# Routing the last tokens of a fused attention, dense and expert kernel in halves, one turned by TensorE

## The chip, the cores and the metric

The kernel runs on 1 core of one Trainium2 chip. The metric is the device time of one execution in microseconds; the number given is the median of several runs. A span is the time from the first to the last instruction of the profiled execution.

## What is computed

Three layers in a row. Attention over 2 batches x 8 heads x 768 tokens of 64, masked to keys in the query's hash bucket; then a dense layer `g = h * sigmoid(1.702 h)`, `g @ w_out` on 1536 tokens of 512 (hidden 2048); then a layer of 8 experts, two for each token:

```python
logits = x @ w_gate
noise_scale = np.log1p(np.exp(x @ w_noise))
noisy_logits = logits + noise_scale * noise
top2 = np.argpartition(-noisy_logits, 2, axis=1)[:, :2]
...
        h = np.maximum(x[mask] @ w1[e], 0.0)
        out[mask] += top2_w[mask, k, None] * (h @ w2[e])
```

The second and third layer's matmuls are done as three f16 products each (high and low parts).

## The kernel before

**Chunks and steps.** The 1536 tokens form 6 chunks of 256 (`B * NCH`, 3 a batch), each two tiles of 128 (`CT`). The program is one long list of steps. In the first part a step g does one attention tile (g under `NU` = 96) and, for a finished chunk, one of 16 pieces of the dense layer: 8 pieces h (24 matmuls of 256 columns) and 8 pieces px (12 matmuls of 512), 4 for each tile. Chunk 4 is in step 85 + i, chunk 5 in step 99 + i. A table by step (`at`, `start`, `soon`, with offsets from PARAM) says which side work is emitted in which step: loads, weight splits, routing. In a step, `start` work comes first, then the eviction of the last piece (th on ACT and DVE), the matmuls of this piece (`moe_pe`), the split of gt, and last the `at` work, whose generators are run in turns, one instruction each. Every engine runs its own instructions in exactly the order in which they are emitted; nothing overtakes.

**Routing.** When px of a tile is done, ACT and DVE write it as high and low parts to `xr` (L485, L494). `r_t` (L567) turns a tile by a DMA transpose on SP's queue into `xrt`. `route` (L572) is a generator: 16 small matmuls pz, a copy zc on ACT, some 35 DVE operations on tiles of 128 x 16 or less with four exponentials on ACT between them, the choice of two experts (top, ix), the one-hot mk, two matmuls pp that count the tokens ahead of each in its expert (cum carries the sum over chunks), and slot numbers si. It ends with four indirect DMAs on POOL's queue (L685), a tile and choice each, that scatter the rows of `xr` with their metadata into `slots` in DRAM. It yields between instructions, and `yield 1` where the result goes to another engine. `next` or `piece` takes it to the next `yield 1`: before, one or two a step. `reserve` (L693) sees to it that the first 256 slots of expert 0 hold only tokens of chunks 0 to 4, so that they can be loaded before chunk 5 is routed.

**Experts.** In the second part a step x is one item of a list: "1" a group of 12 matmuls into ph (`l1`, L790; the first weights times a block of hidden units), with its eviction to ht by ACT and DVE one step later, or "2" a tile of 24 matmuls into py (`l2`, L813). Expert 0 (`EA` = 1) has two parts: slots 0 to 255, then 256 to 399. `e_load` (L749) loads a part's tokens by a transposing DMA from `slots` into xg, on SP's queue, and the metadata mt; `e_meta` (L769) turns mt into weights and row numbers by six or more small DVE operations. `w12_load` and `w12_split` (L724, L735) load an expert's weights in 512 KB blocks and split them on ACT and DVE. The order on PE is: 8 groups ph and 2 tiles py of expert 0's first part, 8 groups ph of its second part, the first group ph of expert 1, then py and ph in turns to the end.

**Chunk 5 before.** Its routing is not in the table: from x = 2 on, up to 8 instructions of its generator are emitted ahead of each expert step (`QX` = 8, `QS` = 2), and it has to be done at x = 7 (`QE`), where expert 0's second part is loaded:

```python
    for x in range(-4, len(seq) + 2):
        for _ in range(PARAM["QX"]):
            if x >= PARAM["QS"]:
                next(gen, None)
```

Names of tiles in the rows are those of the program; L numbers are lines of the kernel before.

Of the kernel before, what the change touches and what calls it, by code (L numbers as in the profile page):

```python
# [7 lines left out]
F32 = mybir.dt.float32  # L8
# [10 lines left out]
DM = H * D  # L19
# [37 lines left out]
PARAM.update(KA={(0, 0, 0): -15, (0, 0, 1): -6, (0, 1, 0): -5, (0, 1, 1): -4, (0, 2, 0): -1, (0, 2, 1): 1, (0, 3, 0): 4, (0, 3, 1): 5, (1, 0, 0): 37, (1, 0, 1): 39, (1, 1, 0): 44, (1, 1, 1): 46, (1, 2, 0): 42, (1, 2, 1): 51, (1, 3, 0): 47, (1, 3, 1): 51}, QA={(0, 0, 0): -15, (0, 0, 1): -3, (0, 0, 2): 1, (0, 0, 3): 3, (0, 1, 0): 8, (0, 1, 1): 9, (0, 1, 2): 17, (0, 1, 3): 21, (0, 2, 0): 24, (0, 2, 1): 28, (0, 2, 2): 30, (0, 2, 3): 33, (1, 0, 0): 37, (1, 0, 1): 41, (1, 0, 2): 47, (1, 0, 3): 52, (1, 1, 0): 57, (1, 1, 1): 56, (1, 1, 2): 60, (1, 1, 3): 69, (1, 2, 0): 72, (1, 2, 1): 69, (1, 2, 2): 80, (1, 2, 3): 84}, VA={(0, 0, 0): -1, (0, 0, 1): -3, (0, 1, 0): -1, (0, 1, 1): -1, (0, 2, 0): 0, (0, 2, 1): 0, (0, 3, 0): -1, (0, 3, 1): -2, (1, 0, 0): -1, (1, 0, 1): -1, (1, 1, 0): 2, (1, 1, 1): -4, (1, 2, 0): -3, (1, 2, 1): -3, (1, 3, 0): 2, (1, 3, 1): -2}, PV={(0, 0, 0): 4, (0, 0, 1): 5, (0, 0, 2): 6, (0, 0, 3): 5, (0, 1, 0): 6, (0, 1, 1): 4, (0, 1, 2): 4, (0, 1, 3): 5, (0, 2, 0): 5, (0, 2, 1): 5, (0, 2, 2): 5, (0, 2, 3): 6, (1, 0, 0): 4, (1, 0, 1): 5, (1, 0, 2): 4, (1, 0, 3): 5, (1, 1, 0): 5, (1, 1, 1): 5, (1, 1, 2): 5, (1, 1, 3): 6, (1, 2, 0): 6, (1, 2, 1): 4, (1, 2, 2): 4, (1, 2, 3): 4}, RA={0: 18, 1: 18, 2: 19, 3: 24, 4: 18}, W=[(g,1) for g in [-6, -4, -3, -1, 0, 0, 1, 1, 2, 4, 4, 7, 8, 8, 9, 10, 11, 12, 13, 14, 15, 16, 16, 17, 18, 20, 20, 22, 22, 23, 23, 24]], EC=lambda g:'AA', LE=lambda nc:nc.sync, HI=lambda g:'AAAA'[g%4], LO=lambda g:[0, 0, 0, 1, 0, 0, 0, 1][g%8]==1, S1=[8, 8, 8, 8, 8, 11, 13, 22], ST={0: 4, 1: 4, 2: 5, 3: 4, 4: 5, 5: 3}, NG=28, WS=lambda i:'PAAA'[i%4], HE=lambda nm,b:'DPDD'[2*(nm=='k')+b], OE=lambda nm,b:'DTDD'[2*(nm=='k')+b], SC=lambda nm,b:'DADD'[2*(nm=='k')+b], R1=2, I0=26, IS=1, O0=56, OS=1, GM=100, BK=3, OH=3, QX=8, QS=2, QE=7, VF=0, T0=12, T1=17, EL=10, WX=5, WL=2, PC=2, GW=2, E0=8, WB=2)  # L57
# [3 lines left out]
def fused(ctx: ExitStack, tc: tile.TileContext, q, k, v, proj, w_in, w_out, w_gate, w_noise, noise,  # L61
# [505 lines left out]
    def r_t(ci, t):  # L567
        xrt = rt.tile([128, 2 * HP, 128], U16, name="xrt")
        rst[ci, "xt", t] = xrt.bitcast(F16)
        nc.sync.dma_start_transpose(xrt, mst[ci, "xr"][:, t, :2 * DM])  # L570

    def route(ci):  # L572
        b, cc = divmod(ci, NCH)
        pz = psr.tile([128, CT, 4 * E], F32, name="pz", tag="pb", bufs=1)
        for t in range(CT):
            xrt = rst.pop((ci, "xt", t))
# [13 lines left out]
        w = rt.tile([128, 6, CT, E], F32, name="rw", bufs=1)  # L590
# [22 lines left out]
        nc.vector.tensor_tensor(y, y, noi[:, b, cc * CT:(cc + 1) * CT, :], op=OP.mult)  # L613
# [547 lines left out]
```

## Time and profile before

| | |
|---|---|
| three runs | 814.7, 815.28, 812.03 us; median 814.7 |
| the profiled execution | 813.59 us, span 811.9 us |
| busy, share of the span | PE 705.7 us (87%), DVE 536.6 (66%), ACT 446.0 (55%), POOL 270.3 (33%) |
| mean granted TensorE clock | 0.956 of full speed |
| costliest group | L460, PE, h: 1152 matmuls, 142.5 us |

The profile is of one execution. Each row of its timeline gives start, duration, engine, line, operation, output and inputs, and in brackets how long the engine had been idle and on what it waited. The chain of waits follows the work that ended last backwards, at each step to what released it. PEclk is the clock granted to TensorE as a share of 2.4 GHz; 0.50 is its other level, 1.2 GHz.

### The profile page before, as it was taken

The numbers are of one execution on the slowest core, as the hardware profiler recorded it, in microseconds if no ns is written. First come the engines' busy times: TensorE is split into PE (matmuls) and PEld (weight loads), VectorE is DVE, ScalarE is ACT, GpSimd is POOL, SyncE is SP. The second block draws the span as 40 slices with busy tenths as digits, with TensorE's granted clock in tenths as the row PEclk, the third lists the DMA queues.
The fourth block names the chain that finished last, engine by engine and source line by source line (L and its number), as shares of the span: only waits on it lengthen the run. The fifth ranks groups of instructions, "written<-read, shape, count | busy, mean of one in ns | idle before, by whom it ended". The sixth has DMA issues, their size and how long they took to land.

```text
span 811.9 us, 14841 instructions
## 1 busy us (share of the span) xinstructions
PE 705.7 (87%) x5398; PEld 436.7 (54%) x5399; DVE 536.6 (66%) x1338; ACT 446.0 (55%) x859; POOL 270.3 (33%) x305
## 2 busy tenths in 40 slices
PE   1576578988988888889899999897999999999995
PEld 1353346645754565468468667365545545555452
DVE  8999789996896789569778724563635436354320
ACT  3678767766876686467567615342534435344220
POOL 6444646561444054304212223231130211302113
PEclk9979679899999999999999999998999999999998
DMA  8999679999999999996796650858768768587313
GB/s 220 216 250 236 177 173 188 253 265 237 179 163 205 166 189 194 210 171 105 119 182 119 111 182 12 208 197 210 169 173 216 161 181 206 128 203 156 79 17 45
DMA packets 267998, 139.46 MB, mean 172 GB/s; under 512 B 225232, under 2 KB 243728, under 8 KB 267920
## 3 DMA queue, kind: packets, MB, share of 16 engines
q1 hardware_dynamic: 261904, 125.31, 69.5%
q0 software_dynamic: 6016, 13.16, 9.0%
q8 instruction: 43, 0.70, 0.4%
q14 instruction: 35, 0.29, 0.1%
HBM read 61.48 MB, written 23.20 MB: 104 GB/s over the span
## 4 chain that ended last, share of the span: by engine, by line
PE 45%; DVE 23%; DMA 15%; issue 7%; ACT 6%; POOL 3%; SPq 1%; POOLq 0%; ACTq 0%; DVEq 0%
PE ph L799 16%; PE py L830 14%; PE h L460 5%; PE px L471 5%; DMA et<-er 5%; DVE er L323 4%; DVE e L266 3%; DMA qt<-qsb 3%; ACT er L314 2%; DMA q<-in_q_dram 2%; DMA qt<-qsa 2%; DVE wf L431 2%; DVE wraw L434 2%; ACT e L275 2%; PE s L254 2%
## 5 line engine op out<-in xcount | busy, mean ns | idle before, releaser
L460 PE MATMUL h<-xt,wi 128*128 128x256 f16 x1152 | 142.5, 279 | 6.9 <-DVE th L490 3.0
L799 PE MATMUL ph<-xg,ew 128*128 128x400 f16 (+2 forms) x864 | 136.4, 322 | 8.8 <-DMA xg<-slots 8.7
L743 DVE SCALAR_TENSOR_TENSOR ew<-w,ew 128x1024 f16<-128x1024 f32 x64 | 77.9, 1225 | 82.2 <-ACT ew L742 82.1
L471 PE MATMUL px<-wo,gt 128*128 128x512 f16 x576 | 131.0, 379 | 0.5 <-DVE th L490 0.5
L460 PEld LDWEIGHTS <-wi 128*128 128x128 f16 x1152 | 113.7, 100 | 29.8 <-issue 9.8
L830 PE MATMUL py<-ew,ht 128*128 128x512 f16 x576 | 125.8, 379 | 0.0
L847 POOL DMA_INDIRECT out_dram<-yo,ti x32 | 54.0, 1687 | 204.8 <-ACT yo L840 197.9
L254 PE MATMUL s<-kt,qt 128*128 128x512 f16 (+1 forms) x384 | 86.9, 348 | 35.0 <-DVE mx L266 28.0
L799 PEld LDWEIGHTS <-ew 128*128 128x128 f16 x864 | 83.7, 102 | 59.9 <-issue 6.8
L275 ACT ACTIVATE e<-e,mx 128x768 f32<-128x768 f32 x96 | 89.4, 931 | 28.7 <-DVE mx L266 22.0
L505 POOL TENSOR_TENSOR gt<-th,gt 128x512 f16<-128x512 f32 x48 | 59.3, 1236 | 123.5 <-ACT gt L504 123.0
L266 DVE CUSTOM_DVE_ANT_0 e<-s,zero 128x768 f32<-128x768 f32 x96 | 90.6, 948 | 6.5 <-PE pt L293 2.6
L323 DVE SCALAR_TENSOR_TENSOR er<-e,mx,er 128x768 f16<-128x768 f32 x68 | 73.5, 1083 | 28.9 <-ACT er L314 28.3
L830 PEld LDWEIGHTS <-ht 128*128 128x128 f16 x576 | 56.3, 98 | 67.0
L471 PEld LDWEIGHTS <-gt 128*128 128x128 f16 x576 | 54.9, 98 | 62.6 <-issue 0.8
L314 ACT ACTIVATE er<-e,mx 128x768 f16<-128x768 f32 x68 | 63.1, 930 | 40.7 <-DMA et<-er 26.7
L809 ACT ACTIVATE ht<-ph 128x400 f16<-128x400 f32 (+2 forms) x72 | 33.5, 466 | 72.8 <-PE ph L799 72.7
L254 PEld LDWEIGHTS <-qt 128*128 128x128 f16 x384 | 36.9, 102 | 64.0 <-issue 37.4
L742 ACT ACTIVATE ew<-w 128x1024 f16<-128x1024 f32 x64 | 66.4, 1048 | 3.7 <-DMA w<-in_moe_w_dram 3.4
L840 ACT ACTIVATE yo<-py,wv 128x512 f32<-128x512 f32 x24 | 16.5, 686 | 90.2 <-PE py L830 57.3
L810 DVE SCALAR_TENSOR_TENSOR ht<-ph,ht 128x400 f16<-128x400 f32 (+2 forms) x72 | 37.6, 523 | 36.7 <-ACT ht L809 36.7
L368 PE MATMUL pv<-et,vt 128*64 128x256 f16 x720 | 50.3, 281 | 5.4 <-DMA et<-er 5.4
(197 smaller groups left out, 932.3 us busy)
## 6 DMA issues: line engine op xcount, KB each, us to landing
w<-in_moe_w_dram SPq DMA_DIRECT2D x64, 512.0 KB, 4.7
wraw<-in_moe_w_in_dram SPq DMA_DIRECT2D x16, 512.0 KB, 4.5
wraw<-in_moe_w_out_dram SPq DMA_DIRECT2D x16, 512.0 KB, 4.2
slots<-blank SPq DMA_DIRECT2D x6, 1032.0 KB, 6.8
v<-in_v_dram SPq DMA_DIRECT2D x24, 192.0 KB, 4.1
out_dram<-zeros SPq DMA_DIRECT2D x13, 256.0 KB, 3.3
k<-in_k_dram SPq DMA_DIRECT2D x16, 192.0 KB, 3.8
q<-in_q_dram SPq DMA_DIRECT2D x24, 128.0 KB, 3.1
```

What stands on the lines that cost most here:

```text
L254: nc.tensor.matmul(ps[:, n0 * 128:n1 * 128], qt[:, s, h, t, :], kt[:, s, h, n0:n1, :].rearrange("p c t -> p (c t)"), start=(s == 0), stop= ...
L266: nc.vector.tensor_tensor_reduce(e32, st[g]["ps"][:, :S], zero.to_broadcast([128, S]), -0.125, TOP, op0=OP.add, op1=OP.min, accum_out=mx[: ...
L275: nc.scalar.activation(e32, e32, AF.Exp, scale=-1.0, bias=st[g]["mx"][:, 1:2], accum_out=sms[b, cc, hp][:, 2 * h + t:2 * h + t + 1] if g < ...
L314: nc.scalar.activation(er[:, 0], st[g]["e"], AF.Copy, scale=r)
L323: nc.vector.scalar_tensor_tensor(er[:, 1], d["e"], d["mx"][:, 3:4], er[:, 0], op0=OP.mult, op1=OP.subtract)
L460: nc.tensor.matmul(ph[:, a, :], wi[ws][:, d, f0:f0 + 128], xt[:, d, xs, :], start=(d == 0 and ws == 0 and xs == 0), stop=(d == HP - 1 and ...
L471: nc.tensor.matmul(px, gts[ci, f // 2][:, gs, f % 2, t * 128:t * 128 + 128], wo[ws][:, f, :], start=(f == 0 and gs == 0 and ws == 0), stop ...
L505: nc.gpsimd.tensor_tensor(gt[:, 1], th, gt[:, 0], op=OP.subtract)
L742: nc.scalar.activation(hi, x, AF.Copy, scale=SW1 if j == 0 else SW2)
L743: nc.vector.scalar_tensor_tensor(lo, x, SW1 if j == 0 else SW2, hi, op0=OP.mult, op1=OP.subtract)
L799: nc.tensor.matmul(ph[:, :c1 - c0], w[:, ws, d * FE + f * 128:d * FE + f * 128 + 128], xg[e, p][:, xs * HP + d, :], start=(d == 0 and ws = ...
L830: nc.tensor.matmul(py, ht[:, f, hs, t * 128:t * 128 + 128], w[:, ws, f * DM:(f + 1) * DM], start=(i == 0), stop=(i == n - 1))
```

## The change

Four things are changed.

1. **Chunk 4's routing takes more hops a step.** With r0 = 103 it was taken one hop a step from step 103 to 107, its last part (from the exponential d on) in step 110, `reserve` in 111. Now `hops` takes three in step 103, four in 104, one in 105; the last part with the scatters comes in step 107, `reserve` in 108. `e_load` of expert 0 is called one step earlier (112), and `e_meta` later (x = 4, not step 115).
2. **Chunk 5 is routed in two halves** of one tile each, two generators `gen0` and `gen`, each with its own matmuls, about as many DVE and ACT operations as a whole chunk, and two scatters. `gen0` starts in step 114; its small tiles are cut out of one tile zt. `gen` is emitted from x = 3, in turns with the rest of `gen0`.
3. **The second half's rows are turned by TensorE**: 8 transposes (128x128, f16) into a PSUM tile xp, emitted at x = 1 behind the second ph group, and two copies of 128x512, one on ACT, one on DVE. The DMA transpose of that tile is gone from SP's queue.
4. In PARAM, `QX` goes from 8 to 10 and `QS` from 2 to 3 (a line that is not shown).

The core of the diff; in `route` all other lines change only in that `CT` becomes `T`, `rt.tile` becomes `small`, and a slice is cut to the half:

```diff
-        nc.sync.dma_start_transpose(xrt, mst[ci, "xr"][:, t, :2 * DM])
-
-    def route(ci):
+        xr = mst[ci, "xr"][:, t, :2 * DM]
+        if (ci, t) != LAST:
+            nc.sync.dma_start_transpose(xrt, xr)
+            return
+        xp = psum2.tile([128, 2 * HP, 128], F16, name="xp", bufs=1)
+        for i in range(2):
+            for d in range(i * HP, i * HP + HP):
+                nc.tensor.transpose(xp[:, d], xr[:, d * 128:d * 128 + 128].bitcast(F16), ident)
+            o = xrt[:, i * HP:i * HP + HP].bitcast(F16)
+            if i == 0:
+                nc.scalar.activation(o, xp[:, :HP], AF.Copy)
+            else:
+                nc.vector.tensor_copy(o, xp[:, HP:])
+
+    LAST = B * NCH - 1, CT - 1
+
+    def route(ci, ta=0, tb=CT):
         b, cc = divmod(ci, NCH)
-        pz = psr.tile([128, CT, 4 * E], F32, name="pz", tag="pb", bufs=1)
-        for t in range(CT):
-            xrt = rst.pop((ci, "xt", t))
+        T, ts = tb - ta, slice(cc * CT + ta, cc * CT + tb)
+        own = ta == 0 and T < CT
+        if own:
+            zt, used = moe.tile([128, 512], F32, name="zt", tag="wf", bufs=1), [0]
...
+        if (ci, ta) == LAST:
+            pz = psum2.tile([128, T, 4 * E], F32, name="pz", tag="py")
+        else:
+            pz = psr.tile([128, T, 4 * E], F32, name="pz", tag="pb", bufs=1)
+        for t in range(T):
+            xrt = rst.pop((ci, "xt", ta + t))
...
+    def hops(gen, n):
+        for _ in range(n):
+            for x in gen:
+                if x:
+                    break
+                yield
             yield
...
+        if ci == B * NCH - 1:
+            gen0, gen = route(ci, 0, 1), route(ci, 1, 2)
+            for i, n in ((15, 1), (16, 3), (17, 5)):
+                at(g0 + i, hops, gen0, n)
+            continue
         at(g0 + PARAM['T1'], r_t, ci, 1)
         gen = route(ci)
-        if ci < B * NCH - 1:
+        if ci == B * NCH - 2:
+            r0 = g0 + PARAM["RA"].get(ci, PARAM["R0"])
+            start(r0, next, gen)
+            for i, n in ((0, 3), (1, 4), (2, 1)):
+                at(r0 + i, hops, gen, n)
+            start(r0 + 4, next, gen)
+            at(r0 + 4, piece, gen)
+            at(r0 + 5, done, gen)
+            at(r0 + 5, reserve)
+            for e in range(EA):
+                at(r0 + 9, e_load, e, 0)
+        else:
...
-            if ci == B * NCH - 2:
-                at(r0 + 6 + r1, done, gen)
-                at(r0 + 6 + r1, reserve)
-                for e in range(EA):
-                    at(r0 + PARAM["E0"] + r1, e_load, e, 0)
-                    at(r0 + PARAM["E0"] + 2 + r1, e_meta, e, 0)
...
+    at(1, r_t, *LAST)
+    for e in range(EA):
+        at(4, e_meta, e, 0)
+    at(2, hops, gen0, 1)
...
             if x >= PARAM["QS"]:
                 next(gen, None)
+                next(gen0, None)
```

How the order of instructions changes. Lines of the changed kernel are 1 to 33 higher: th is L490 and L491, the weight split L743 and L776, ht L810 and L843, si L679 and L713.

First, DVE at the end of chunk 4's routing, before. ew is a split of expert 0's weights; d, xr, cum, ps, ov, oh, sf are the last part's small tiles; si holds the slot numbers for which the scatters wait.

```order
L743 SCALAR_TENSOR_TENSOR ew<-w_6323,ew 128x1024
L655 TENSOR_SCALAR d_6654<-d_6654 128x2
L657 RECIPROCAL xr<-d_6654 128x2
L659 TENSOR_TENSOR xr<-xr,d_6654 128x2
L661 TENSOR_TENSOR cum<-cum,mk 128x8
L665 TENSOR_TENSOR ps__6714<-pq,iota_e 128x16
L667 SCALAR_TENSOR_TENSOR ov<-pq,iota_e 128x16
L670 TENSOR_TENSOR ps__6714<-ps__6714,ov 128x16
L673 TENSOR_TENSOR oh<-oh,ps__6714 128x2x8 x2
L676 TENSOR_REDUCE sf<-oh 128x4
L679 CAST si<-sf 128x4
L494 SCALAR_TENSOR_TENSOR xr<-px,xr 128x512
```

The same place now:

```order
L491 SCALAR_TENSOR_TENSOR th<-th,h 128x512 x2
L776 SCALAR_TENSOR_TENSOR ew<-w_6317,ew 128x1024
L689 TENSOR_SCALAR d_6600<-d_6600 128x2
L691 RECIPROCAL xr<-d_6600 128x2
L693 TENSOR_TENSOR xr<-xr,d_6600 128x2
L695 TENSOR_TENSOR cum<-cum,mk 128x8
L699 TENSOR_TENSOR ps__6666<-pq,iota_e 128x16
L701 SCALAR_TENSOR_TENSOR ov<-pq,iota_e 128x16
L704 TENSOR_TENSOR ps__6666<-ps__6666,ov 128x16
L707 TENSOR_TENSOR oh<-oh,ps__6666 128x2x8 x2
L710 TENSOR_REDUCE sf<-oh 128x4
L713 CAST si<-sf 128x4
```

The last part stood behind the fourth split; now it stands behind the first, with the other three and the eviction of xr behind it.

Second, DVE in chunk 5's routing, before, from the last of e_meta's operations (wv) on; z and rw are the routing's tiles:

```order
L782 TENSOR_TENSOR wv<-wv 128x2
L810 SCALAR_TENSOR_TENSOR ht<-ph,ht 128x256
L586 TENSOR_TENSOR z<-zc 128x32
L592 SCALAR_TENSOR_TENSOR rw<-z 128x16
L597 TENSOR_SCALAR rw<-rw 128x16
L599 TENSOR_SCALAR rw<-rw 128x16
L601 TENSOR_TENSOR rw<-rw 128x16
```

Now, from the first half's mk on (zt are the first half's tiles, xrt<-xp is the copy of the turned rows, z and rw belong to the second half):

```order
L667 TENSOR_TENSOR mk<-zt 128x8
L674 COPY xr<-tok 128x1
L676 COPY xr<-zt 128x1
L679 TENSOR_TENSOR zt<-zt 128x1
L843 SCALAR_TENSOR_TENSOR ht<-ph,ht 128x256
L583 COPY xrt<-xp 128x512
L843 SCALAR_TENSOR_TENSOR ht<-ph,ht 128x256
L689 TENSOR_SCALAR zt<-zt 128x1
L619 TENSOR_TENSOR z<-zc 128x16
L691 RECIPROCAL xr<-zt 128x1
L625 SCALAR_TENSOR_TENSOR rw<-z 128x8
L693 TENSOR_TENSOR xr<-xr,zt 128x1
```

The first half's chain up to mk, some 17 operations, now stands ahead of the first ht and of the copy of the turned rows; behind them the two halves alternate.

Third, ACT at the start of the expert part, now. Before, xr<-px was followed directly by ht, then zc.

```order
L616 ACTIVATE zt<-pz 128x32
L486 ACTIVATE xr<-px 128x512
L628 ACTIVATE zt<-zt 128x8
L638 ACTIVATE zt<-zt 128x8 x2
L842 ACTIVATE ht<-ph 128x256
L581 ACTIVATE xrt<-xp 128x512
L842 ACTIVATE ht<-ph 128x256
L682 ACTIVATE zt<-zt 128x1
L687 ACTIVATE zt<-pp 128x8
L616 ACTIVATE zc<-pz 128x32
```

The first half's copy of pz stands ahead of the eviction of the last px, and its three exponentials ahead of the first ht and of the copy of the turned rows. On PE the first half's 8 pz matmuls stand behind the last px and ahead of the first ph; its pp pair and the second half's pz stand behind the third ph group, the second half's pp pair behind the sixth. On SP and POOL the order stays, but for the transpose that is gone.

## Rows read from the trace of the kernel before

**Rows 1.** The page's first line.

```profile
span 811.9 us, 14841 instructions
```

**Rows 2.** The chain of waits around the two token loads: start, us, link.

```profile
517.43 3.93 DMA slots<-xr,si
521.38 4.07 DMA xg<-slots
525.50 4.26 PE ph L799 x24
...
544.61 4.17 DMA slots<-xr,si
548.80 4.90 DMA xg<-slots
553.74 10.97 PE ph L799 x108
```

**Rows 3.** PE's timeline: start, us, line, operation, count.

```profile
513.69 7.93 PE L471 MATMUL px<-wo,gt 128*128 128x512 f16 x36
...
530.00 5.40 PE L799 MATMUL ph<-xg,ew 128*128 128x256 f16 x48
...
538.42 10.52 PE L830 MATMUL py<-ew,ht 128*128 128x512 f16 x48
```

**Rows 4.** Windows: length, busy PE, PEld, DVE, ACT, POOL, then PEclk, DMA, GB/s.

```profile
571.30:801.30 230.00, 229.92 (x1461) 120.40 (x1461) 98.56 (x169) 91.33 (x131) 48.21 (x56) 1.00 0.64 151
...
553.70:558.00 4.30, 4.26 (x36) 4.26 (x36) 2.46 (x12) 1.52 (x3) 0.00 (x0) 0.50 1.06 233
...
335.50:337.00 1.50, 0.00 (x0) 0.00 (x0) 0.00 (x0) 0.00 (x0) 0.00 (x0) 1.00 1.07 354
337.00:341.00 4.00, 3.54 (x35) 3.04 (x35) 2.99 (x6) 0.94 (x1) 0.75 (x1) 0.57 1.52 268
```

**Rows 5.** PE's groups by form, 525 to 565 us: count, busy us, mean ns, idle.

```profile
L799 PE MATMUL ph<-xg,ew 128*128 128x144 f16 x96 | 8.9, 274 | 4.8 <-DMA xg<-slots 4.8
```

**Rows 6.** Timeline of all engines in chunk 4's routing.

```profile
496.31 0.69 DVE L490 SCALAR_TENSOR_TENSOR th<-th,h 128x512 f32<-128x512 f32 x1 [1.56 <-ACT th L478]
...
499.54 0.17 DVE L607 TENSOR_TENSOR rw<-rw 128x16 f32<-128x16 f32 x1
...
501.20 0.16 DVE L622 FIND_INDEX8 ix<-top,rw 128x8 uint32<-128x8 f32 x1
...
512.57 0.17 DVE L679 CAST si<-sf 128x4 int32<-128x4 f32 x1
```

**Rows 7.** Timeline of all engines in chunk 5's routing.

```profile
522.29 0.69 DVE L494 SCALAR_TENSOR_TENSOR xr<-px,xr 128x512 f16<-128x512 f32 x1 [3.73 <-ACT xr L485]
...
530.44 0.19 DVE L586 TENSOR_TENSOR z<-zc 128x32 f32<-128x32 f32 x1 [1.32 <-ACT zc L583]
...
535.35 0.17 DVE L633 TENSOR_TENSOR mk<-oh 128x16 f16<-128x16 f32 x1
...
537.98 0.17 DVE L679 CAST si<-sf 128x4 int32<-128x4 f32 x1
...
538.92 0.95 POOL L685 DMA_INDIRECT slots<-xr,si  x1 [19.44 <-DVE mt L764]
...
540.18 1.86 POOL L685 DMA_INDIRECT slots<-xr,si  x1 [0.22 <-issue]
```

**Rows 8.** PE's groups by form, 0 to 200 us: a matmul against the identity.

```profile
L352 PE MATMUL pv<-ident,r 128*64 128x128 f16 x56 | 4.6, 266 | 4.8 <-DVE r L342 4.6
```

**Rows 9.** DVE's groups by form: the same 128x512 from PSUM to f16.

```profile
L494 DVE SCALAR_TENSOR_TENSOR xr<-px,xr 128x512 f16<-128x512 f32 x12 | 8.2, 685 | 9.2 <-ACT xr L485 9.1
```

**Rows 10.** Instructions on si, 540 to 541 us: landing of the scatter issued at 540.18.

```profile
DMA to landing us min/median/max: 6.0/6.0/6.0
```

**Rows 11.** Instructions on xg, 552 to 556 us: expert 1's load and its landing.

```profile
L756 SPq DMA_TRANSPOSE xg<-slots x1: 5050/5050/5050, 553.2 to 553.2; - x1
...
DMA to landing us min/median/max: 7.1/7.1/7.1
```

More of the change, by code (lines that the diff above doesn't have):

```diff
@@ L1 @@
+import math
 from contextlib import ExitStack
@@ L581, in route @@
                                  stop=(d == HP - 1))
-        zc = rt.tile([128, CT, 4 * E], F32, name="zc", bufs=1)
+        zc = small([T, 4 * E], F32, "zc")
         nc.scalar.activation(zc, pz, AF.Copy, scale=1.0 / (SX2 * SWG))
         yield 1
-        z = rt.tile([128, CT, 2 * E], F32, name="z", bufs=1)
+        z = small([T, 2 * E], F32, "z")
         nc.vector.tensor_tensor(z, zc[:, :, :2 * E], zc[:, :, 2 * E:], op=OP.add)
@@ L588, in route @@
         zn = z[:, :, E:]
-        w = rt.tile([128, 6, CT, E], F32, name="rw", bufs=1)
+        w = small([6, T, E], F32, "rw")
         ab, t1, y, ex, nl, rel = (w[:, i] for i in range(6))
@@ L616, in route @@
         yield
-        top = rt.tile([128, CT, E], F32, name="top", bufs=1)
-        ix = rt.tile([128, CT, E], U32, name="ix", bufs=1)
-        for t in range(CT):
+        top = small([T, E], F32, "top")
+        ix = small([T, E], U32, "ix")
+        for t in range(T):
             nc.vector.max(top[:, t], nl[:, t])
@@ L643, in route @@
         yield
-        d1 = rt.tile([128, CT, 2], F32, name="d1", bufs=1)
+        d1 = small([T, 2], F32, "d1")
         nc.vector.tensor_tensor(d1[:, :, 0:1], top[:, :, 1:2], top[:, :, 0:1], op=OP.subtract)
@@ L648, in route @@
         nc.scalar.activation(d1[:, :, 0:1], d1[:, :, 0:1], AF.Exp)
-        pp = psr.tile([128, CT, E], F32, name="pp", tag="pb", bufs=1)
-        nc.tensor.matmul(pp, before, mk[:, ci], start=True, stop=False)
-        nc.tensor.matmul(pp, ones, cum, start=False, stop=True)
-        pq = rt.tile([128, CT, E], F32, name="pq", bufs=1)
+        pp = psr.tile([128, T, E], F32, name="pp", tag="pb", bufs=1)
+        nc.tensor.matmul(pp, before, mks, start=True, stop=False)
+        nc.tensor.matmul(pp, ones, cum[:, :T], start=False, stop=True)
+        pq = small([T, E], F32, "pq")
         nc.scalar.activation(pq, pp, AF.Copy)
@@ L674, in route @@
             yield
-        sf = rt.tile([128, CT, 2], F32, name="sf", bufs=1)
+        sf = small([T, 2], F32, "sf")
         nc.vector.tensor_reduce(sf, oh, axis=AX.X, op=OP.add)
         yield
-        si = rt.tile([128, CT, 2], I32, name="si")
+        si = small([T, 2], I32, "si", 2)
         nc.vector.tensor_copy(si, sf)
         yield
-        xr = mst.pop((ci, "xr"))
-        for t in range(CT):
+        for t in range(T):
             for c in range(2):
```

45 lines of the change are left out of this document (28 added, 17 removed).

## The prediction

> **What bounds the kernel now.** I read the profile in this order: the chain that ended last, the stages by window, the PE timeline around the hand-over from the dense layer to the experts, then the instructions of the two last routings. The profiled execution spans 811.9 us [rows 1] and counts as 813.59 us with what lies around it; that is 1.1 us under the median of the three runs (814.7). The chain shows two places where PE is not the link: indirect DMA, then the transposing load of expert 0's tokens, then PE, once before 525.50 and once before 553.74 [rows 2]. PE's last px matmul ends at 513.69 + 7.93 = 521.62 [rows 3], so the first wait is 3.88 us. The last py block of expert 0's first part ends at 538.42 + 10.52 = 548.94 [rows 3], so the second wait is 4.80 us. From 571.3 to 801.3 PE is busy for 229.92 of 230 us at the full clock [rows 4]: whatever is gained before 564 reaches the end whole. Both waits cost more than their length: behind the second the granted clock is 0.50, the 1.2 GHz level [rows 4], and behind the first 24 matmuls of 256 columns took 4.26 us [rows 2]; warm, 48 took 5.40 [rows 3], so 24 take 2.70. The 96 matmuls of 144 columns after the second wait took 8.9 us [rows 5]; warm, by their columns, 144/256 x 112.5 ns x 96 = 6.1 us. Waits and slow matmuls together are 3.88 + 1.56 + 4.80 + 2.8 = 13.0 us, the most that the change can get.
>
> **Chunk 4 in more hops a step.** Its last part moves from step 110 to 107; a step of 12 px matmuls takes 2.64 us (36 in 7.93 [rows 3]), so slot numbers si come up to 7.9 us earlier than 512.57 [rows 6]. One weight split still stands ahead of that part on DVE, behind a delayed th, and I take 5 us. Everything behind si follows: the last scatter landed at 517.43 + 3.93 = 521.36, the load at 525.45 [rows 2]; now about 520.4. That is before PE is free, so the first wait goes, with some 1.5 us to spare. No queue is in the way: POOL and SP keep their order, but for one DMA transpose that leaves SP. The price: in step 104 nine to ten small DVE operations stand between two th operations; before, the same run took from 499.54 to 501.36 [rows 6]. The th that was at 496.31 [rows 6] then ends at about 498.5, half a microsecond after the matmul that needs its PSUM buffer; cost 0 to 1, taken as 0.5. px ends at 522.1.
>
> **Chunk 5, first half.** Its 8 pz matmuls stand on PE behind all px matmuls, so it starts at 522.1 however early its rows were turned. On ACT the copy of pz goes ahead of the eviction of xr, so xr, complete at 522.98 before [rows 7], is complete at about 523.8, and the DVE chain starts there. A whole chunk needs from z (530.44) to mk (535.52) 5.1 us [rows 7]. Half a chunk has one max pair fewer and none of the three ht operations in between; its operations are as many and each about as long. I take 4.2 us: mk at 528.0.
>
> **Chunk 5, second half, turned by TensorE.** PE reaches the 8 transposes behind two ph groups at 522.1 + 0.2 + 2.7 = 525.0. The trace has no f16 transpose; the nearest are matmuls of 128 columns against the identity, 56 in 4.6 us [rows 8], so 0.65 us, 1.3 at half clock. Two copies of 128x512 follow; DVE's nearest row is 0.685 us [rows 9]. But the copies queue: DVE's stands behind the whole first half's chain and one ht operation, so it runs from 528.8 to 529.5. PE meanwhile finishes a third ph group at 527.0, waits for the first half's mk until 528.1, then for the DVE copy until 529.5. So pz of the second half is done at about 529.6, hardly before the old pz, which ended where the next ph began, at 530.00 [rows 3]. From there the old chain took until 537.98 + 0.17 = 538.15 [rows 7], 8.15 us. Now the first half's last twelve operations and six of e_meta are woven in; I add 1.2 us (bounds 0 and 2): si at 539.0. PE waits for the second mk from 533.6 to about 536.1, and the py block ends at 549.5. **The first wait is thus not saved but moved into two waits on mk and xrt.**
>
> **The last scatters.** Here is the gain. POOL has two scatters behind that si, not four: the second goes out 1.26 us after the first [rows 7], at 540.3, where the fourth went at 544.61 [rows 2]. Landing takes 4.17 [rows 2] to 6.0 us [rows 10]; I take 5.0: 545.3. The load then lands 4.90 later [rows 2], at 550.2; PE waits 0.7 instead of 4.80. Its 96 matmuls end warm at 556.3. The next expert's load was issued 4.38 us after this one, at 553.18 [rows 2, 11], and took 7.1 us [rows 11]: now 545.35 + 4.38 + 7.1 = 556.8. So the matmuls of expert 1, which started at 553.74 + 8.9 = 562.6 [rows 2, 5], start at 556.8: **5.8 us earlier**, with bounds of 4.8 and 6.6 from the two landings alone and 3.5 to 7.5 with those of si. What is late next is the token load of expert 1. The half-clock risk is covered: if the wait at 528 or 535 drops the clock, as 1.5 us without a matmul did at 335.5 (0.57 in the 4 us behind it, [rows 4]), a slower third to fifth ph group fills time that PE would spend waiting for mk; only py would lose, up to 2 us, and of that 1.2 are time that PE would otherwise spend waiting for the two loads.
>
> The sum on the profiled execution is 813.59 - 5.8 = 807.8; on the median it is 808.9. I give 808.3.
>
> **Rivals.**
> *Both waits really go.* If TensorE's turn is not held in DVE's queue (the small operations half as wide being clearly shorter), pz is done at 527.0, si follows 8.15 us later at 535.2, scatters land at 541.5, the two loads at 546.4 and 553.0; the gain is 9.6 us: 804.0, and 801 if no wait were left at all. For it: the route from xr to xrt has only three short operations. Against it: the order on DVE, and that an operation on 128x8 has no shorter row than one on 128x16. The Trainium skill, page "VectorE: DVE Perf Modes", section "The three transpose paths", gives TensorE 390 ns for a 128x128 transpose and the DMA crossbar 1309 ns, and its rules for authors send such a transpose to TensorE if PSUM will do; by that the time would be this rival's 804.0. No run here shows a TensorE transpose of this type yet, and the trace bears out the speed but not the place in the queue.
> *The chain is slower still.* Eight times the two woven chains pass between DVE and ACT, where ht operations and exponentials are queued; if this costs 3 us more, or the two scatters land late, si and all behind it shift one for one: gain about 2.5, 811 to 812. For it: PE waits at both pp places, so a late ht also holds ph groups. Against it: two chains fill each other's gaps.
> *Slower.* The transposes now stand on PE behind ph groups that need expert 0's first load; the DMA transpose did not. If that load is late, the whole second half is late. Up to some 524 it costs nothing. At 525.5, its old time, two cold ph groups put the transposes at 529.8 and si at 542: gain still 2.9. Every microsecond beyond is lost one for one, so from about 528.5 the kernel is slower, and by 4 us from 532.5. For it: the four scatters of chunk 4 now run beside the 512 KB weight loads. Against it: the 5 us taken above, and even without them the load was there at 525.45 [rows 2].
>
> **How the numbers follow.** A measurement of this kernel can tell about 0.5%, 4.1 us, from no change: faster means under 810.6. Forecast 0.60 (806.5 to 810.5), both waits gone 0.13 (801 to 806), slower chain 0.22 (810.5 to 814), slower 0.05. Faster is nearly all of the first and the second, 0.70; same is the third and the edges, 0.26; slower 0.04. The range leaves out half of the second case and the far ends: 803.5 to 812.5.
>
> **What would show it.** Right: the first ph matmul within 1 us of px's end; PE idle in front of pp and pz between 526 and 537, some 4 to 5 us in all; si of the last half at 538 to 540; its second scatter near 540; a wait of 0 to 2 us before each of the next two token loads. Wrong: pz of the second half done before 528 (then 804), si past 541 (then 811 and more), or ph waiting for expert 0's first load beyond 525 (then slower).

## The result and the profile after

The changed kernel took 818.59 us (median of 10 runs, 815.95 to 823.09), the kernel before 814.65 beside it; the ratio is 1.0057, with a 95% interval of 1.0034 to 1.0079. The forecast was 808.3 with 803.5 to 812.5: by the ratio it is some 4.6 us slower (3.9 by the medians), not 6 us faster.

The profiled execution, the fastest of the ten, spans 814.2 us (815.95 with what lies around it). The dense part ahead of the change is up to 3.7 us shorter or longer from one profile to the next: chunk 4's first pz matmul stands at 489.78 us before and at 489.11 after, and in the kernels below between 488.40 and 492.09. So I compare **the stretch** from that matmul to the first ph matmul behind pc (the one small matmul that sums up the counts of all tokens, at 571.25 us before), where PE begins to be busy without a gap. It is 571.29 - 489.78 = 81.51 us before and 573.82 - 489.11 = 84.71 after: 3.20 us longer. It shows where the time of one execution went; whether a kernel is faster is for the medians and ratios.

The chain of waits of the changed kernel, the part that answers to [rows 2]; columns are start, us, link:

```profile
523.64 0.69 DVE xr L495
524.43 2.78 PE ph L832 x24
...
527.47 0.60 ACT xrt L581
528.12 0.38 PE xp L578 x4
...
540.68 9.27 PE py L863 x43
549.95 13.04 DMA xg<-slots
563.12 4.12 PE ph L832 x12
```

Both pairs of scatter and load that stood in [rows 2] are gone from the chain, as the prediction said. In their place stands one load of 13.04 us: expert 1's. PE's timeline shows what the wait took:

```profile
498.82 2.78 PE L461 MATMUL h<-xt,wi 128*128 128x256 f16 x24 [1.29 <-DVE th L491]
...
524.43 2.78 PE L832 MATMUL ph<-xg,ew 128*128 128x256 f16 x24 [1.54 <-DVE zt L619]
...
528.12 0.38 PE L578 MATMUL xp<-ident,xr 128*128 128x128 f16 x4 [0.69 <-ACT xrt L581]
...
529.70 0.25 PE L611 MATMUL pz<-wg,xrt 128*128 128x32 f16 x4
...
536.16 0.18 PE L684 MATMUL pp<-mk,before 128*128 128x8 f16 x1 [2.13 <-DVE mk L667]
...
536.23 4.45 PE L832 MATMUL ph<-xg,ew 128*128 128x256 f16 x24
540.51 10.52 PE L863 MATMUL py<-ew,ht 128*128 128x512 f16 x48
550.87 3.16 PE L832 MATMUL ph<-xg,ew 128*128 128x144 f16 x48
554.59 3.23 PE L832 MATMUL ph<-xg,ew 128*128 128x144 f16 x48 [0.55 <-DVE ht L843]
563.12 4.12 PE L832 MATMUL ph<-xg,ew 128*128 128x400 f16 x12 [5.31 <-DMA xg<-slots]
```

Expert 0's second part starts at 550.87 without waiting for its load. Then PE stands 5.31 us for expert 1's, and the 12 matmuls behind that take 4.12 us: in the window 563.1 to 567.2 the granted clock is 0.52. What else was under way at the time, from the timelines of SP and POOL:

```profile
544.93 1.95 SPq L789 DMA_TRANSPOSE xg<-slots  x1
...
549.46 0.39 SPq L764 DMA_DIRECT2D w<-in_moe_w_dram  x1
549.95 5.89 SPq L789 DMA_TRANSPOSE xg<-slots  x1
...
549.03 1.90 POOL L880 DMA_INDIRECT out_dram<-yo,ti  x1 [7.51 <-ACT yo L873]
...
552.04 1.59 POOL L880 DMA_INDIRECT out_dram<-yo,ti  x1 [1.07 <-ACT yo L873]
```

And the DMA view of 553.2 to 561.2: GB/s in 40 slices, then each queue's packets, MB and share of 16 engines:

```profile
GB/s 238 271 278 229 212 210 200 164 165 157 188 239 236 285 284 242 95 26 37 40 26 172 232 202 133 116 129 140 173 191 168 82 91 83 77 78 272 115 238 320
q1 hardware_dynamic: 3317, 0.83, 88.2%
q0 software_dynamic: 283, 0.52, 40.2%
xg<-slots SPq DMA_TRANSPOSE x1, 13.0
```

q1 is SP's load of 400 rows with small loads of mt, q0 POOL's two scatter-adds of expert 0's first output tiles into out. For eight microseconds the packets of both lie beside each other, at 171 GB/s for the two together. The scatter-adds landed after 10.0 and 10.2 us. In the kernel before they stood here in POOL's timeline:

```profile
547.31 1.90 POOL L847 DMA_INDIRECT out_dram<-yo,ti  x1 [1.66 <-ACT yo L840]
...
549.94 1.59 POOL L847 DMA_INDIRECT out_dram<-yo,ti  x1 [0.69 <-ACT yo L840]
```

They landed in 5.3 and 5.0 us. The load went out at 553.18, its packets began about 556, after theirs had ended near 555, and it took 7.1 us [rows 11].

### The profile page after: what moved, and what is told of

It is laid out like the page before. It is cut to its first block, busy times and chain, and to the rows that moved or that the text cites. A ratio compares the mean times of both kernels' runs of the same rounds, so it can differ in the third digit from the quotient of the medians.

```text
span 814.2 us, 14902 instructions
## 1 busy us (share of the span) xinstructions
PE 705.3 (87%) x5408; PEld 434.8 (53%) x5409; DVE 541.1 (66%) x1368; ACT 446.9 (55%) x866; POOL 268.0 (33%) x305
## 4 chain that ended last, share of the span: by engine, by line
PE 43%; DVE 6%; DMA 3%; ACT 2%; issue 1%; POOL 0%; POOLq 0%; ACTq 0%; DVEq 0%
PE ph L832 15%; PE py L863 15%; PE px L472 7%; PE h L461 2%; DMA xg<-slots 2%; DVE er L324 1%; PE py L857 1%; PE pv L369 1%; DMA et<-er 1%; DVE th L491 1%; PE s L255 1%; ACT er L315 1%; DVE e L267 1%; DMA qt<-qsa 0%; POOL out_dram L880 0%
## 5 line engine op out<-in xcount | busy, mean ns | idle before, releaser
L776 DVE SCALAR_TENSOR_TENSOR ew<-w,ew 128x1024 f16<-128x1024 f32 x64 | 78.0, 1225 | 83.4 <-ACT ew L775 83.4
L832 PEld LDWEIGHTS <-ew 128*128 128x128 f16 x864 | 81.7, 99 | 59.1 <-issue 9.2
L843 DVE SCALAR_TENSOR_TENSOR ht<-ph,ht 128x400 f16<-128x400 f32 (+2 forms) x72 | 37.5, 524 | 36.4 <-ACT ht L842 36.4
```

What stands on the lines that cost most here:

```text
L776: nc.vector.scalar_tensor_tensor(lo, x, SW1 if j == 0 else SW2, hi, op0=OP.mult, op1=OP.subtract)
L832: nc.tensor.matmul(ph[:, :c1 - c0], w[:, ws, d * FE + f * 128:d * FE + f * 128 + 128], xg[e, p][:, xs * HP + d, :], start=(d == 0 and ws = ...
```

## Experiments

Each set of kernels ran beside the kernel before on the same chip; the ratio is to that. There are four sets, on different chips (e1, e2, e3, e5; e4, e6, e7, e8; e9 to e12; e13 to e15), so that kernels of two sets are compared by ratios and stretches, not by medians. The stretch is worked out as above, from one execution each.

| kernel | median us | ratio (95%) | stretch, against before |
|---|---|---|---|
| changed kernel | 818.59 | 1.0057 (1.0034 to 1.0079) | +3.20 |
| e1: scatter-adds later | 809.93 | 0.9954 (0.9935 to 0.9973) | -3.55 |
| e2: before, scatter-adds later | 813.28 | 0.9992 (0.9972 to 1.0013) | -2.23 |
| e6: scatter-adds two steps later | 813.36 | 0.9963 (0.9943 to 0.9982) | -0.97 |
| e7: load right behind the other | 818.88 | 1.0035 (1.0014 to 1.0055) | +3.06 |
| e8: the same, on before | 823.47 | 1.0099 (1.0072 to 1.0126) | +7.12 |
| e9: e7, work on mt late | 817.43 | 1.0049 (1.0030 to 1.0067) | +7.99 |
| e3: hops only | 812.29 | 0.9991 (0.9971 to 1.0011) | -1.38 |
| e4: halves and turn only | 821.67 | 1.0060 (1.0041 to 1.0079) | +4.69 |
| e5: DMA turn | 817.95 | 1.0035 (1.0011 to 1.0059) | +4.18 |
| e12: e4, scatter-adds later | 812.76 | 0.9984 (0.9965 to 1.0004) | -1.34 |
| e13: hops, scatter-adds later | 812.76 | 0.9972 (0.9953 to 0.9991) | -3.12 |
| e10: e1, weights early | 809.71 | 0.9946 (0.9925 to 0.9967) | -4.24 |
| e11: e9, weights early | 812.65 | 0.9986 (0.9965 to 1.0007) | -2.92 |
| e14: e13, weights early | 811.43 | 0.9930 (0.9902 to 0.9958) | -4.03 |
| e15: e10, DMA turn | 808.72 | 0.9909 (0.9887 to 0.9931) | -5.29 |

### Do the load and the scatter-adds slow each other?

**e1** moves the copies and scatter-adds of two tiles; no other work moves. wv and ti get a third buffer, since they now live longer.

```diff
             k_, *a = seq[x - 1]
-            (l1_out if k_ == "1" else l2_out)(*a)
+            if k_ == "2" and (a[0], a[1]) == (0, 0):
+                at(18, l2_out, *a)
+            else:
+                (l1_out if k_ == "1" else l2_out)(*a)
```

> The changed kernel, with the copies and scatter-adds of expert 0's first two output tiles moved on, behind the last ht of its second part (some 558 us), so that they no longer run beside expert 1's token load. Theory A (load and scatter-adds slow each other): the load is issued near 550 as now, lands in about 7 us instead of 13.0, so expert 1's first matmul starts near 557 instead of 563.1 and its 12 matmuls take about 2.2 us instead of 4.12; time 809 to 812 us, against 818.6 for the changed kernel. Theory B (the load is slow for another reason: weight loads beside it, or rows read right behind the last scatters): landing 12 us or more, start near 563, time 817 to 820.

Measured 809.93 us, ratio 0.9954. The DMA view of 553.5 to 557 in e1:

```profile
GB/s 445 360 319 310 325 261 293 260 176 246 287 293 287 287 295 281 301 287 290 293 281 298 290 287 295 281 301 287 287 287 290 298 290 287 295 278 164 259 19 10
q1 hardware_dynamic: 3420, 0.94, 117.0%
xg<-slots SPq DMA_TRANSPOSE x1, 6.4
```

Alone, the load moves at an even 290 GB/s and lands in 6.4 us; the weight load ahead of it (550.46) and the rows just scattered are as they were. PE, in e1's timeline, no longer waits for it; the 60 matmuls hold the last 48 of expert 0's second part and expert 1's first 12:

```profile
541.44 10.52 PE L863 MATMUL py<-ew,ht 128*128 128x512 f16 x48
551.80 3.35 PE L832 MATMUL ph<-xg,ew 128*128 128x144 f16 x48
555.59 5.29 PE L832 MATMUL ph<-xg,ew 128*128 128x144 f16 x60 [0.44 <-DVE ht L843]
```

Theory A holds and B falls: the ratio goes from 1.0057 to 0.9954, some 8 us, by moving two scatter-adds. At their new place, 560.03 and 561.96, they took 8.8 and 8.1 us beside weight loads, but there nothing waited for them.

**e2** is the converse, at(11), that is step x = 11, in the kernel before.

> The converse on the kernel before: its two scatter-adds of expert 0's first tiles, which there have landed when expert 1's load is issued at 553.2, are moved two and one steps later, to about 555 to 558, right onto that load; nothing else moves. Theory A: the load lands in 10 to 13 us instead of 7.1, expert 1 starts at 564 to 567 instead of 562.6, time 2 to 6 us above that of the kernel before (816.5 to 820.5). Theory B: landing 7 us, time as before, 814.7 within 1.

Theory A's number was missed: time and landing are those of theory B. The timelines of SP and POOL, and the DMA view of 553.7 to 557 and of 557 to 560, say why:

```profile
551.39 4.09 SPq L756 DMA_TRANSPOSE xg<-slots  x1
...
553.29 1.62 POOL L847 DMA_INDIRECT out_dram<-yo,ti  x1 [9.23 <-ACT yo L840]
...
555.22 1.59 POOL L847 DMA_INDIRECT out_dram<-yo,ti  x1 [0.27 <-issue]
```

```profile
q1 hardware_dynamic: 3278, 0.95, 119.4%
q0 software_dynamic: 20, 0.04, 6.7%
xg<-slots SPq DMA_TRANSPOSE x1, 7.4
...
q0 software_dynamic: 265, 0.48, 89.6%
q1 hardware_dynamic: 583, 0.13, 22.4%
```

Here the first packets of a scatter-add move 3.5 us after its issue (2.4 in the kernel before, 4.6 in the changed kernel). Issued 1.9 us behind the load, they stood beside it by issue times but followed it by packets: 20 of them before 557, 265 after. Load 7.4 us, scatter-adds 5.4 and 5.6. So this run made no collision and says nothing against A: issues that lie close together are not enough, the packets have to meet. The miss shows a second thing: the load of 144 rows, with nothing beside it, landed in 3.2 us instead of 4.90 [rows 2].

**e6** tried to separate the two readings with at(11) in the changed kernel.

> The changed kernel with the two scatter-adds moved on by two steps alone, so that they are issued about 2 and 4 us behind the issue of expert 1's load and run beside it. In the run on the kernel before where they were issued 1.9 and 3.8 us behind the load, the load took 7.4 and they 5.4 and 5.6 us. Theory A1 (any overlap slows both): load 10 to 13 us, expert 1 starts at 561 or later, time 816 to 819. Theory A2 (it matters that a scatter-add is issued within about a microsecond ahead of the load, so that both are at their start together): load 7 to 8 us, expert 1 starts at 558, time 809.5 to 812.5. Theory B (the load is slow by itself here): 13 us, 818.

Ratio 0.9963. The scatter-adds went out 4.25 and 6.45 us behind the load (554.54), and only 15 of their packets lie ahead of 561.5, where the load's had ended near 560.4. The time, 813.36 us, is a little above that of theory A2, and the load had no collision; so it does not tell A1 from A2, and no other run settles it: wherever most of expert 1's load met their packets (the changed kernel, e4, e5, e8, e9), a scatter-add had also been issued within a microsecond ahead of it.

**e8** forces the collision on the kernel before, **e7** avoids it in the changed kernel, both with one edit:

```diff
             at(b0, done, gen)
-            at(b0, e_load, e, p)
-            at(b0 + 1, e_meta, e, p)
+            at(b0, e_load_x, e, p)
+            at(b0, e_load_x, e + 1, 0)
+            at(b0, e_load_m, e, p)
+            at(14, e_meta, e, p)
```

> The same move on the kernel before: expert 1's load is issued near 550.2 instead of 553.18, that is 0.2 us behind the second scatter-add (549.94) instead of 3.2 behind. Theories A1 and A2: the load takes 10 to 13 us instead of 7.1 and the second scatter-add 8 to 10 instead of 5.0, so that the load lands at 560 to 563 all the same; time within 1.5 us of the kernel before. Theory B: 7 to 8 us, landed at 558; no later than before, time 814 to 815, since PE is busy with expert 0's second part until 562.6.

> The changed kernel with expert 1's token load issued right behind that of expert 0's second part, ahead of the five small mt loads and one weight load that stood between them: about 546.9 instead of 549.95, some 2 us ahead of the first scatter-add (549.0) instead of 0.9 behind it. Theory A1 (any overlap slows): 10 to 13 us, landed 557 to 560, time 810.5 to 814. Theory A2 (only a scatter-add just ahead of the load): the load takes 7 to 9 us, two loads being in flight, and is there before PE wants it near 557.8, scatter-adds land in 5 to 6 us; time 809 to 812. Theory B: 13 us, landed 560, 813 to 815.

In e8 the two loads went out from 547.52 on, between the scatter-adds at 546.04 and 548.55: from 552 to 557, with scatter-add packets beside them, they moved 70 to 150 GB/s, and 280 in the microsecond after, alone. In e7 the loads (from 546.64) were through near 555, and the scatter-adds' packets began at 554. That is as theory A has it; but neither time came out: 823.47 us where 1.5 us about the kernel before was expected, 818.88 where 809 to 814 was. I first laid that to DVE's wait for the mt loads, which now came late, and **e9** moved that work behind expert 0's second part (at(18) for both e_meta).

> As the kernel with expert 1's load right behind that of expert 0's second part, but the work on DVE that waits for the small mt loads (weights and token numbers of both) moved on by four and three steps, behind the last ht of expert 0's second part, since in that kernel DVE stood 4.9 us in front of it and PE with it. Theory A (packets of a load and of scatter-adds that really lie beside each other slow both): the load's packets are over near 554, before those of the scatter-adds begin; no wait for it, none on ht beyond 1 us; expert 1 starts near 558; time 808 to 811.5. If the late mt loads still hold something (expert 0's third tile is scaled by them), 812 to 815.

It got no better: 817.43 us where 808 to 811.5 was expected. The loads went out later here, the second at 551.1 behind a scatter-add at 550.88, and took 3.6 and 9.1 us, the scatter-adds 9.1 and 7.9, so that the collision was not avoided either. But PE did not wait for expert 1's load. The DVE timelines of e8 and e9 show what it had been:

```profile
563.89 1.22 DVE L743 SCALAR_TENSOR_TENSOR ew<-w,ew 128x1024 f16<-128x1024 f32 x1 [5.52 <-ACT ew L742]
```

```profile
565.36 1.23 DVE L776 SCALAR_TENSOR_TENSOR ew<-w,ew 128x1024 f16<-128x1024 f32 x1 [8.14 <-ACT ew L775]
```

Not mt: the one 512 KB weight load that I had pushed behind the token load on SP's queue (issued at 557.51 in e9, landing 6.7 us). ACT waits 8.18 us for it (4.85 in e7), ACT and DVE stand at its split, the ht operations behind them, and PE behind those. My reading in e9's expectation was wrong. With six weight buffers (e11, below) the stop is gone.

### What each part of the change is worth

**e3** is the kernel before with the table of hops of chunk 4, **e4** the changed kernel with the old pieces for chunk 4, **e5** the changed kernel with dma_start_transpose for every tile.

> The kernel before with chunk 4's faster routing alone; chunk 5 is routed whole and turned by the DMA engines as before. The first wait for a load goes; px ends at 522.5 to 523; chunk 5's si comes at 536 to 538, its fourth scatter 6.4 us later, the load of expert 0's second part lands near 552, expert 1's load is issued near 551. Theory A: the two scatter-adds go out near 540 and 545 and have landed by then, so the load takes about 7 us and expert 1 starts at 558 to 560: time 810.5 to 813. Theory B: with a load of 13 us it starts at 564: 815 to 818.

> The changed kernel with chunk 4 routed as before: the halves and TensorE's turn alone. The first wait of about 3.9 us stays, ph starts 4.1 us after px's end as before; the transposes stand behind two slow ph groups, si of the last half comes some 1 us later against px's end than in the changed kernel, its second scatter as well. Both readings of the contention, and theory B: expert 1's load is issued within 2 us of the two scatter-adds, 10 to 13 us landing; time 817 to 821, as the changed kernel or worse. If the first routing's price were what made the change lose, this kernel would be at 812 or below.

> The changed kernel, with the last tile turned by a transposing DMA again instead of TensorE. If TensorE's turn is what the halves need: the DMA turn is issued near 523.7 behind expert 0's load on the same queue and lands near 529 or later, pz of the second half is done at 530 to 532 instead of 529.9, si and all behind it 0 to 2 us later; but expert 0's scatter-adds stay at 549 and 552, so that theory A lets the collision with expert 1's load shrink by as much: time 817 to 820, as the changed kernel or 1 us above it. Theory B: 819 to 822, later by the whole shift.

Alone, hops change nothing that can be told (0.9991), and their first wait shrank to 2.73 us instead of going; halves lose 0.6% like the whole change, 821.67 us where 817 to 821 was expected. e4's load was issued 0.6 us behind the second scatter-add (556.17 and 555.59), and expert 1's first matmul followed 12.4 us behind that issue (568.58). Hops alone keep the old order, scatter-adds first, and the load took 7.6 us; in e5 it took 13.1, 0.55 us behind a scatter-add. In e5 pz of the second half begins 0.7 us earlier, counted from chunk 4's first pz, than with TensorE's turn (531.51 - 491.66 = 39.85 against 529.70 - 489.11 = 40.59): the turn was not what the second half waited for.

With the collision taken away, the parts can be told apart: **e12** is e4 and **e13** is e3, each with e1's edit.

> The halves and TensorE's turn alone (chunk 4 routed as before), with the two scatter-adds moved behind expert 0's second part: tells what chunk 4's hops are worth once the collision is gone. If the first wait that they take away is worth its length (3.75 us of wait and 1.5 to 2.5 us of slow matmuls against 1.5 to 2.2 us of wait, less 1.3 us for the delayed th): 2 to 3 us above the kernel with hops, 812 to 813.5. If the first wait is only moved into the waits on mk and on the turn, as the prediction had it: 810 to 811. Theory A is borne out by either, against 821.7 without the move.

> Chunk 4's hops alone (chunk 5 whole, four scatters behind its si, turned by the DMA engines), with the two scatter-adds moved behind expert 0's second part. If the halves carry the gain, as the prediction's step on the last scatters had it: four scatters still stand behind si, the wait for the load of expert 0's second part stays near 3 us (4.55 with hops alone, less 1.4 us since nothing lies beside that load any more), ratio about 0.997, 811.5 to 813. If the halves are worth nothing: ratio 0.9954 as both together, 809.5 to 811.

e12 fell into its first case: hops are worth 2.2 us beside the halves by the stretch (80.17 to 77.96 us, e12 to e1) and 2.4 by the ratio, though these intervals overlap a little. e13 has the wait and the ratio of its first case as well, but the halves carry little: beside the hops they are worth 0.4 us by the stretch (78.39 to 77.96, e13 to e1) and 0.0018, or 1.5 us, by ratios whose intervals overlap. PE's timeline of e13 says why the halves are worth so little:

```profile
538.07 10.52 PE L830 MATMUL py<-ew,ht 128*128 128x512 f16 x48
551.77 6.29 PE L799 MATMUL ph<-xg,ew 128*128 128x144 f16 x72 [3.18 <-DMA xg<-slots]
```

Without halves py ends 538.07 + 10.52 - 490.55 = 58.0 us behind chunk 4's first pz and PE then waits 3.18 us; with them (e1) py ends at 541.44 + 10.52 - 489.49 = 62.5 and PE waits for nothing, yet starts the second part later (62.3 against 61.2). The wait on the scatters was exchanged for those on mk and on the turn in front of py.

### With two more weight buffers

**e10** adds two weight buffers to e1 (w32 from 4 to 6), so that two of the four loads at step 107 and behind go out some 35 us earlier (473.50 in e10, 506.39 in the changed kernel):

```diff
-    for i in range(4):
+    for i in range(6):
         at(NU + 3, w12_load, 0, i)
     for i in range(8):
         at(NU + 11 + i, w12_split, 0, i)
-        if i < 4:
-            at(NU + 11 + i, w12_load, 0, i + 4)
+        if i + 6 < 8:
+            at(NU + 11 + i, w12_load, 0, i + 6)
```

> The kernel with the two scatter-adds moved behind expert 0's second part, and two of the four 512 KB weight loads that run beside chunk 4's four scatters issued some 25 us earlier (six buffers instead of four). If the scatters land in 6 to 7.5 us (3.7 to 5.7 before) because of those loads, the last lands in about 5, expert 0's load is there 1 to 2 us earlier, PE waits about 1.5 us for PSUM alone and stays at the full clock: 1 to 2 us under the kernel with the scatter-adds moved, 808 to 809.5. If they are slow for another reason (the transposing turn of chunk 5's first half beside them, or a scatter ahead of them), landing 6 to 7.5 as now and time as that kernel's, 810 within 1.

> Both other moves together: expert 1's load right behind the one before it, the work that waits for mt late, and two weight loads early. If both work as their theories say, 807.5 to 810; if the weight loads make no difference, as the kernel with the load right behind and the work on mt late.

The landing of chunk 4's last scatter, in the DMA view of the changed kernel (issued at 513.24) and of e10 (issued at 515.48):

```profile
slots<-xr,si POOLq DMA_INDIRECT x1, 6.7
```

```profile
slots<-xr,si POOLq DMA_INDIRECT x1, 3.5
```

The weight loads were the reason. Expert 0's load is issued 519.00 - 491.36 = 27.6 us behind chunk 4's first pz instead of 519.95 - 489.11 = 30.8, and ph then waits for PSUM alone (1.50 us). The gain over e1, 0.7 us by the stretch, is less than the comparison can tell; by the landing it is the first case, by the time, 809.71 us, it can be either. e11 lost the stop at the split, but with 812.65 us it missed both its cases and is behind e1 and e10: PE still waits 1.21 us for ht in expert 0's second part.

**e14** gives e13 the same buffers, **e15** gives e10 the DMA turn.

> The same, and two of the weight loads beside chunk 4's scatters issued earlier. If the scatters land in 3.5 us as they did with the halves, expert 0's load is there about when px ends, the first wait (2.7 us with hops alone) shrinks to 0 to 1.6, and the whole chunk's si comes as much earlier unless its turn by the DMA engines sets it: 809 to 811.5 by the one, 811.5 to 813 by the other. Against 0.9946 with the halves: the difference is what the halves and TensorE's turn are worth with everything else out of the way.

> The kernel with halves, hops, scatter-adds later and two weight loads early (0.9946), its last tile turned by a transposing DMA instead of TensorE. If TensorE's turn has no part in it, as in the changed kernel (0.7 us earlier pz with the DMA turn): 0.993 to 0.997. If it has, since now the queue is free of the wait for chunk 4's scatters: pz 1 to 2 us later, 0.996 to 0.998.

e14 fell into its first case, and it is level with e10 (0.9930 against 0.9946): in the form that the change has, with TensorE's turn, the halves are worth nothing here that can be told (0.2 us by the stretch, 1.3 the other way by the ratio).

e15 is the fastest: 808.72 us (five runs), ratio 0.9909, its interval below 1 and below that of the changed kernel. The ratio lies under both its cases; pz came 1.1 us earlier, not later. Its SP and PE timelines:

```profile
518.21 2.20 SPq L778 DMA_TRANSPOSE xg<-slots  x1
...
525.71 4.10 PE L821 MATMUL ph<-xg,ew 128*128 128x256 f16 x36 [1.50 <-DVE xr L495]
...
529.88 0.25 PE L600 MATMUL pz<-wg,xrt 128*128 128x32 f16 x4
...
554.81 5.25 PE L821 MATMUL ph<-xg,ew 128*128 128x144 f16 x60 [0.55 <-DVE ht L832]
```

With nothing ahead of the DMA turn on SP, pz begins 529.88 - 490.42 = 39.5 us behind chunk 4's first pz, 1.1 earlier than with TensorE's turn: PE does its three ph groups in one piece, where in the changed kernel the turn holds it from 527.04 to 528.34 between the second and the third. The halves are then worth 1.3 us by the stretch and 1.7 by the ratio (e14 to e15), and TensorE's turn costs 1.05 by the stretch (e15 to e10); the intervals of these ratios overlap, so that neither is settled.

## Why the prediction was wrong

**The step that failed** is in the part on the last scatters: "The next expert's load was issued 4.38 us after this one, at 553.18, and took 7.1 us: now 545.35 + 4.38 + 7.1 = 556.8." The issue was right: 549.95 measured against 549.7 (549.1 when 0.67 us are taken off, by which chunk 4's first pz is earlier in the changed kernel's profile). The landing was 13.04 us, not 7.1. The 7.1 came from a place where expert 0's scatter-adds were 3.2 us ahead of the load. The change moved the load 3.2 us forward and the scatter-adds 1.7 to 2.1 us back, since py came later: the two met. No rival had this; all kept that landing. e1 shows that it is the meeting that costs; e8 shows slow loads beside scatter-adds on the kernel before as well, though its time is for the most part that of the late weight load. Of the 9.0 us between the forecast (-5.8) and the stretch (+3.2), expert 1's start 7.0 us late makes seven (563.12 against 556.8 - 0.67) and the half clock behind the wait the other two: 12 matmuls took 4.12 us, and 2.19 without a lowered clock in e4.

**Chunk 4 in more hops.** si came at 508.0; predicted 507.6, or 506.9 with those 0.67 us off. The delayed th cost 1.29 us of PE instead of 0.5, in every kernel with hops (1.28 to 1.29) and in none without: two small DVE operations ahead of it took 1.12 us instead of 0.17 (last section); no run tried that by itself. That the first wait goes was half wrong: 1.54 us of 3.88 stayed, 1.4 to 2.7 in the other kernels with hops. Expert 0's load was expected about 520.4 and was there at 519.95 + 4.3 = 524.25, because the last scatter landed in 6.7 us, not in the 3.93 of [rows 2], beside weight loads. It is the same fault as the big one, a landing carried over to another neighbourhood; and the text had the neighbours, in the rival on the other side, which needed the load at 528.5 to decide and did not come about. PSUM was not priced at all: ph waits for the bank that the last px leaves when DVE has read it (1.54 us; the row names the operation behind that on DVE, the chain and e15's row name xr L495, which ph does not read).

**First and second half.** Right: PE waits on mk until 536.16, predicted 536.1. Right in the number alone: pz of the second half at 529.70, predicted 529.6. The prediction had PE there by 527.0 and waiting 2.5 us for the first half's mk and for DVE's copy; in the run the first ph came 2.1 us late and the turn held PE for another 1.3, 0.69 of it in the middle of the eight transposes for ACT's copy, so that PE reached pp and pz when mk and the copy were there and waited for neither. The waits are thus 0.69 and 2.13 us, 2.8 where 4 to 5 were named, and TensorE's turn does stand in the chain to pz. Luck as well is the second scatter at 540.47, predicted 540.3: si came at 538.44 instead of 539.0, and the sum had left out the 0.77 us between si and POOL's first scatter, 538.15 and 538.92 in [rows 7]. Right that TensorE's turn gains nothing. The Trainium skill, page "VectorE: DVE Perf Modes", section "The three transpose paths", ranks TensorE ahead of the DMA crossbar by a factor of three. Four transposes of 128x128 took 0.39 us here, as long as the page gives for one, but e5 and e15 put the kernel with the DMA turn level or, not settled, ahead: the place of the turn in PE's and ACT's order outweighed its speed.

**"Here is the gain."** The two scatters fewer did what was said: the load of the second part went out at 544.93, predicted 545.35, and PE did not wait for it. But py ended at 540.51 + 10.52 = 551.03, predicted 549.5 (548.8): behind the wait on mk the granted clock was 0.60 (536.2 to 540.5), and the 24 ph matmuls there took 4.45 us instead of 2.78, which the text bounded at 2 us and took as covered. With the collision away (e1) expert 1 starts 69.2 us behind chunk 4's first pz against a forecast of 556.8 - 489.78 = 67.0. The halves carry 0.4 to 1.7 us of the gain (e13 to e1, e14 to e15) or nothing (e14 to e10), not the 5.8 that the step gave them. And the scatter landed in 2.8 us, not 5.0, so the load could have gone out at 543.3; it was SP that held it. In its waits from 535 to 548, two weight loads ahead of the token load stood for DVE's splits to free a buffer:

```profile
SPq L764 <- DVE ew L776: 17.6, 2, 16.9
```

With six buffers SP waits for the scatter alone, and the load goes out 1.8 us earlier counted from chunk 4's first pz (545.42 - 491.36 = 54.1 in e10, 544.93 - 489.11 = 55.8 in the changed kernel). The prediction moved steps past SP's queue without asking what stood in it.

## What to carry to other kernels

The landing time of a DMA belongs to its neighbours: before carrying it to a new place, list what the order of the other queues puts there, and by when their packets move, which for the scatter-adds here was 2.4 to 4.6 us after their issue. When a load is pulled forward on the critical path, the stores of the stage before it have to be looked at as if they had been moved as well; pushing two of them on by eleven microseconds took some 8 us off the changed kernel.

## What the runs showed of the hardware

**A transposing load and a scatter-add slow each other by more than their bytes.** Alone the load moves 290 GB/s (e1). The scatter-adds of e2 moved 205 GB/s from 557 to 558, alone but for one packet, and 0.48 MB in the 3 us from 557 to 560, 160 GB/s, with 0.13 MB of q1 beside them. Together they moved 171. One behind the other, 0.83 and 0.52 MB would take 0.83/0.29 + 0.52/0.205 = 5.4 us, or 6.1 at 160; together they took 8.0. The Trainium skill, page "DMA: Bandwidth & Descriptors", section "SWDGE vs HWDGE vs iDMA", says that the two kinds of queue feed different queues in each DMA engine, which takes turns between them. The trace agrees in that packets of both queues move in the same microseconds; no run shows where the missing 2 to 2.6 us go.

**A small DVE operation can last as long as a POOL operation.** In the timelines of POOL and DVE of the changed kernel:

```profile
491.87 1.15 POOL L506 TENSOR_TENSOR gt<-th,gt 128x512 f16<-128x512 f32 x1 [1.90 <-ACT gt L505]
494.68 1.16 POOL L506 TENSOR_TENSOR gt<-th,gt 128x512 f16<-128x512 f32 x1 [1.66 <-ACT gt L505]
...
491.93 1.12 DVE L630 TENSOR_SCALAR rw<-rw 128x16 f32<-128x16 f32 x1 [0.49 <-ACT rw L628]
...
494.74 1.12 DVE L640 TENSOR_TENSOR rw<-rw 128x16 f32<-128x16 f32 x1 [0.80 <-ACT rw L638]
...
496.35 0.17 DVE L640 TENSOR_TENSOR rw<-rw 128x16 f32<-128x16 f32 x1 [0.28 <-ACT rw L638]
```

The same operation takes 0.17 us when POOL is idle and 1.12 when it starts 0.06 us behind a POOL operation, ending with it. The Trainium skill, page "SBUF — State Buffer", section "SBUF: two separate sides", has it: the two engines share a port pair that one of them holds for a whole instruction; the trace agrees. It could have been read before: in DVE's groups from 300 to 500 us of the kernel before, the mean of one such form is far above 0.17.

```profile
L613 DVE TENSOR_TENSOR rw<-rw,noi 128x16 f32<-128x16 f32 x3 | 1.4, 472 | 0.0
```
